# The input layer from token 1024 on as Strassen's seven block products, with weight sums streamed from device memory

## The chip, the cores and the metric

The kernel runs on one core of one Trainium2 chip. The metric is device time in microseconds: the median over several executions. A profile is of one execution, and its span runs from the first to the last instruction. Engines are named as in the profile: PE (TensorE matmuls), PEld (TensorE weight loads), DVE (VectorE), ACT (ScalarE), POOL (GpSimd), SP (SyncE, which issues most DMAs).

## The reference

Attention with 8 batches, 8 heads, 576 positions and head size 64, where four heads see a local window of 32 positions and four see positions with the same remainder modulo 32; its output is the input of a layer with three weight matrices, whose maximum goes through an output matrix:

```
scores = where(mask_of_head, (q @ k.T) / sqrt(64), -1e9)
attn   = softmax(scores)
x      = (attn @ v) as (8 * 576 tokens, 8 * 64 features)      # 4608 x 512
h      = maximum(maximum(x @ w1, x @ w2), x @ w3)             # w: 512 x 768
out    = h @ w_out                                            # 768 x 512
```

q, k, v are float32; the weights arrive as float64.

## The kernel before

Precision: TensorE multiplies in a reduced float32 ("float32r"). So each operand is split into a high part (the value rounded to that format) and a low part (what is left), and each product of a 128x128 block of weights with tokens is three matmuls: high x high, high x low, low x high. The weights are turned from 64-bit to 32-bit numbers and split on the chip, in the opening.

Attention is worked in 32 units (8 batches, 4 pairs of heads; pairs 2 and 3 strided, then 0 and 1 local). A unit's steps are `scores` (TensorE), `less_maximum` (DVE: mask, maximum, subtraction), `exponentials` (ACT), `probabilities` and `transposed` (DVE), `values` (TensorE), `leading` (ACT writes the high part of x) and `rest` (DVE writes the low part). From batch 1 on strided units also need `paired_queries`, four ACT copies. `load_qk` and `load_v` issue the unit's loads on SP.

The layer is worked in 9 chunks of 512 tokens, with features on the partitions, so that weights are the stationary operand. For each of 6 column blocks j and each of 3 matrices i, `ff_in` is a group of 12 matmuls (4 blocks of 128 features, three products each) of 512 columns into one of two accumulator banks; `ff_max` then takes it out: a copy by ACT for i = 0, a running maximum by DVE for i = 1 and 2, and then the split of the hidden layer (`hh` by ACT, `hl` by POOL). After the 18 groups `ff_out` makes four output tiles of 128 tokens, 18 matmuls of 512 columns each, which `ff_store` copies and stores.

Chunk 0 and the weights' conversion are in an opening whose order is written out by hand (`OPENING`: a letter for the step, a number for the unit, weight or group). The other chunks are a loop over 22 steps, with a burst of attention at the four steps in `BURSTS`:

```
if i in BURSTS and c < B - 1:
    n = 4 * (c + 1) + BURSTS.index(i)
    coming = n + 1 if n + 1 < len(units) else None
    values(n)
    if coming:
        scores(coming)
    list(load_v(n + 2)); leading(n); rest(n)
```

Each engine runs its instructions in this program order (`pin`); between engines, semaphores wait for data and for free buffers. A matmul group's first weight load carries the wait for its bank.

## Time and profile before

| | |
|---|---|
| median of 3 executions | 704.01 us (701.05 to 705.07) |
| span of the profiled execution | 701.0 us |
| PE busy | 677.7 us, 97% |
| weight loads (PEld) | 556.3 us, 79% |
| DVE, ACT, POOL busy | 295.7, 194.6, 151.1 us |
| moved by DMA | 55.67 MB, mean 79 GB/s |

The profile page has totals by engine, a picture of the span in 40 slices (busy tenths, the clock granted to TensorE, DMA), and the chain that ended last, followed back from the end. Groups of instructions are shown as "line engine operation out<-in shapes xcount | busy us, mean ns of one | idle time before them and who ended it". Answers by time show "start us, us, engine, line, operation".

### The profile page before, as it was taken

What the parts mean: (1) busy time and instruction counts of PE and PEld (TensorE: products, weight loads), DVE (VectorE), ACT (ScalarE), POOL (GpSimd) and SP (SyncE); (2) the same over time, 40 slices, a digit from 0 to 9 for tenths busy, and PEclk for the clock granted to TensorE, in tenths of its full rate; (3) what the DMA queues carried; (4) which work ended last, traced back from release to release, by engine and by line L of the source; (5) the groups of instructions that cost most, each with busy time, mean ns of one, the idle gap of its engine ahead of it and who ended that gap; (6) DMA issues with size and microseconds to landing.
All of it is one profiled execution on the core that took longest, in us unless ns stands there. A gap on an engine that the chain in (4) does not pass through costs nothing.

```text
span 701.0 us, 16767 instructions
## 1 busy us (share of the span) xinstructions
PE 677.7 (97%) x7408; PEld 556.3 (79%) x7408; DVE 295.7 (42%) x505; ACT 194.6 (28%) x440; POOL 151.1 (22%) x153
## 2 busy tenths in 40 slices
PE   3699999999999999999999999999999999999997
PEld 3577878888888888878888888888888888888886
DVE  5886963644435441555145534444255101101110
ACT  4666653212222222122222312222221111111111
POOL 8789880011001100011011100110010101100120
PEclk9999999999999999999999999999999999999999
DMA  8799123211312221222211232223120000010001
GB/s 289 195 291 364 48 84 110 74 56 65 107 54 75 66 81 47 69 84 64 84 56 56 68 108 70 57 65 94 54 54 2 31 31 1 0 46 15 1 1 60
DMA packets 36080, 55.67 MB, mean 79 GB/s; under 512 B 5256, under 2 KB 18568, under 8 KB 36008
## 3 DMA queue, kind: packets, MB, share of 16 engines
q1 hardware_dynamic: 30824, 45.17, 20.9%
q10 hardware_dynamic: 5184, 9.44, 3.6%
q8 instruction: 58, 0.95, 0.6%
q14 instruction: 14, 0.11, 0.0%
HBM read 45.15 MB, written 9.44 MB: 78 GB/s over the span
## 4 chain that ended last, share of the span: by engine, by line
PE 91%; DMA 5%; SPq 2%; DVE 1%; ACT 0%; issue 0%; DVEq 0%; ACTq 0%
PE f_ps L484 62%; PE f_ps L509 21%; DMA w<-in_w 5%; PE o_ps L405 2%; PE o_ps L435 2%; PE s_ps L292 2%; PE s_ps L314 2%; SPq L254 1%; SPq L140 0%; SPq L220 0%; SPq L247 0%; SPq L243 0%; DVE pt L378 0%; DVE s_ps L371 0%; DVE s_ps L368 0%
## 5 line engine op out<-in xcount | busy, mean ns | idle before, releaser
L484 PE MATMUL f_ps<-xh,w 128*128 128x512 f32 x1296 | 409.9, 393 | 0.9 <-ACT h_max L494 0.6
L484 PEld LDWEIGHTS f_ps<-xh,w 128*128 128x128 f32 x1296 | 244.3, 189 | 54.2 <-ACT h_max L494 1.0
L484 PE MATMUL f_ps<-xl,w 128*128 128x512 f32 x648 | 253.6, 391 | 0.4 <-DVE xl L467 0.4
L496 DVE TENSOR_TENSOR h_max<-f_ps,h_max 128x512 f32<-128x512 f32 x108 | 74.3, 688 | 287.9 <-PE f_ps L484 287.9
L500 POOL TENSOR_TENSOR hl<-h_max,hh 128x512 fp32r<-128x512 f32 x54 | 69.6, 1289 | 519.0 <-ACT hh L499 519.0
L484 PEld LDWEIGHTS f_ps<-xl,w 128*128 128x128 f32 x648 | 122.2, 189 | 25.3 <-DVE xl L467 0.7
L509 PE MATMUL f_ps<-wNone,hh 128*128 128x512 f32 x432 | 134.4, 392 | 0.3 <-issue 0.3
L509 PEld LDWEIGHTS f_ps<-wNone,hh 128*128 128x128 f32 x432 | 80.4, 188 | 16.8
L499 ACT CAST hh<-h_max 128x512 fp32r<-128x512 f32 x54 | 33.5, 620 | 202.6 <-DVE h_max L496 202.6
L509 PE MATMUL f_ps<-wNone,hl 128*128 128x512 f32 x216 | 84.1, 389 | 0.0
L467 DVE TENSOR_TENSOR xl<-o_ps,xh 128x320 fp32r<-128x320 f32 (+11 forms) x96 | 28.3, 350 | 53.9 <-ACT xh L463 47.0
L514 ACT COPY work<-f_ps 128x512 f32<-128x512 f32 x36 | 21.2, 589 | 101.5 <-PE f_ps L509 101.5
L494 ACT COPY h_max<-f_ps 128x512 f32<-128x512 f32 x54 | 31.7, 587 | 60.9 <-POOL hl L500 30.0
L509 PEld LDWEIGHTS f_ps<-wNone,hl 128*128 128x128 f32 x216 | 40.5, 188 | 9.1 <-issue 0.5
L358 ACT ACTIVATE s_ps<-s_ps 128x640 f32<-128x640 f32 (+2 forms) x30 | 19.4, 645 | 85.0 <-DVE s_ps L342 85.0
L378 DVE STREAM_TRANSPOSE pt<-s_ps 128x640 f32<-128x640 f32 (+2 forms) x32 | 32.4, 1013 | 0.7
L463 ACT CAST xh<-o_ps 128x320 fp32r<-128x320 f32 (+11 forms) x96 | 24.3, 328 | 25.4 <-PE o_ps L435 19.1
L314 PE MATMUL s_ps<-qk_t 64*32 64x64 f32 (+1 forms) x1408 | 20.0, 232 | 9.8 <-DMA qk_t<-in_kT 7.8
L314 PEld LDWEIGHTS s_ps<-qk_t 64*32 64x32 f32 x1408 | 16.7, 116 | 13.8 <-DMA qk_t<-in_qT 7.8
L337 DVE TENSOR_REDUCE mx<-s_ps 128x10 f32<-128x640 f32 (+2 forms) x32 | 24.7, 772 | 4.3 <-PE s_ps L314 3.3
L371 DVE TENSOR_TENSOR s_ps<-s_ps,sm 128x640 f32<-128x640 f32 (+2 forms) x32 | 25.0, 781 | 1.1
L184 POOL TENSOR_TENSOR work<-work,w 128x512 int32<-128x512 int32 x18 | 23.5, 1313 | 4.2 <-DVE sm L369 2.4
(55 smaller groups left out, 375.5 us busy)
## 6 DMA issues: line engine op xcount, KB each, us to landing
w<-in_w SPq DMA_DIRECT2D x18, 512.0 KB, 5.6
out<-work ACTq DMA_DIRECT2D x36, 256.0 KB, 2.0
qk_t<-in_qT SPq DMA_DIRECT2D x28, 288.0 KB, 3.4
qk_t<-in_kT SPq DMA_DIRECT2D x28, 288.0 KB, 3.6
v_t<-in_v_str SPq DMA_DIRECT2D x56, 128.0 KB, 3.3
v_t<-in_v_loc SPq DMA_DIRECT2D x48, 96.0 KB, 3.1
wNone<-in_w_out SPq DMA_DIRECT2D x6, 512.0 KB, 8.9
qk_t<-in_qk_str SPq DMA_DIRECT2D x4, 288.0 KB, 4.0
```

The lines of the kernel that those rows point to most:

```text
L314: pin(nc.tensor.matmul(s_ps[32 * j : 32 * (j + 1), h, k1 : k1 + w], t[hs, q0 : q0 + 32], t[hs, k0 : k0 + w], start=not first, stop=not fir ...
L337: pin(nc.vector.tensor_reduce(out=mx[:, :, :nm], in_=s, op=ALU.max, axis=axes))
L371: pin(nc.vector.tensor_tensor(out=s, in0=s, in1=wide(sm), op=ALU.mult))
L378: pin(nc.vector.transpose(pt[:, :, : nm * at], s_ps[:, :, : nm * at]))
L463: pin(nc.scalar.copy(out=hi, in_=src))
L467: pin(nc.vector.tensor_tensor(out=lo, in0=src, in1=hi.bitcast(F32), op=ALU.subtract))
L484: pin(nc.tensor.matmul(f_ps, w[:, kc, :], x[:, kc, :], start=(kc == 2 and n == 0), stop=(kc == 1 and n == 2)))
L494: pin(nc.scalar.copy(out=a, in_=f_ps))
L496: pin(nc.vector.tensor_tensor(out=a, in0=f_ps, in1=a, op=ALU.max))
L499: pin(nc.scalar.copy(out=hh, in_=a))
L500: pin(nc.gpsimd.tensor_tensor(out=hl, in0=a, in1=hh.bitcast(F32), op=ALU.subtract))
L509: pin(nc.tensor.matmul(f_ps, h[:, ts], w, start=(j == 0 and n == 0), stop=(j == NJ - 1 and n == 2)))
```

## The change

Chunks 0 and 1 (1024 tokens) stay as they were. The other 3584 tokens are eight blocks of 448; two neighbouring blocks make one of four rounds ("supers"). Within a round the input layer is a product of 2x2 blocks: two halves of the 512 features by two blocks of tokens, and for each matrix two neighbouring column blocks j, j + 1. Of the weights and of the tokens, sums and differences are formed (Strassen's method in Winograd's form), and seven block products of 2 x 3 matmuls of 448 columns take the place of eight. A "quad" (q = 0 to 8) is one pair of column blocks of one matrix: seven products into two accumulator banks that take turns. Each product but one is copied out by ACT (`snap`); a later product goes on adding onto the same bank, which forms part of the sums, and POOL adds the remaining pairs. DVE takes the maximum over the three matrices into one buffer `hall` of the whole round.

The sums of weights are built in the opening's end and in chunk 1 (`build_sums`, `build_mix`, `build_high`, `build_low`: mostly POOL), split in high and low and written to device memory. From there each product's weights (256 KB) are loaded by SP, eight products ahead. Attention's values for tokens from 1024 on, and for chunk 1, are copied whole (float32) by `leading`, without `rest`; `conversion` forms the sums of tokens and splits them during the output tiles of the round before (four pieces, in all seven ACT, nine DVE and two POOL operations 896 columns wide); `chunk_one` splits chunk 1.

Bursts of attention: eight instead of four in chunk 1 (two to three steps apart), then 6, 6, 4 and 0 in the four rounds, one in ten products; `values` and `scores` come ahead of a product, `exponentials` after the third, `probabilities` and `transposed` after the fourth, `paired_queries` after the sixth. `split` takes the place of `hh` and `hl`, partly ahead of the ninth quad's end. The output layer has the same number and size of matmuls.

```
-N7 H6 U8 L6 V7 Q1 Q2 H7 O3 Q3 L7 S8
...
+H5 D21 A23 F15 B22 N6 K22 C20 F16 K23 C21 L5 M15 M16 D22 B23 S7 D23 C22 C23 F17 V6 M17 Y0 X7 O0 G7 Q0 T2 T3 O1 O2
+N7 H6 U8 L6 Z0 V7 S8 Q1 Y1 T0 H7 X8 Q2 O3 E8 L7 T1 Q3 N8
...
+    def chunk_one(p):
+        raw, (hi, lo) = place_of(-1)[:, p, :], (x[:, p, :] for x in x_chunk(1))
+        pin(nc.scalar.copy(out=hi, in_=raw))
+        pin(nc.vector.tensor_tensor(out=lo, in0=raw, in1=hi.bitcast(F32), op=ALU.subtract))
...
+    def build_sums(q):
+        _, j, i = builds[q]
+        to = scratch[q].rearrange("p n (l f) -> p n l f", l=2)
+        for n in range(2):
+            pin(nc.sync.dma_start(out=to[:, A12 : A11 + 1, n], in_=halves(kept[i, j].bitcast(F32)[:, n])))
+        pin(nc.sync.dma_start(out=to[:, A22], in_=kept[i, j + 1].bitcast(F32)[:, :, :256]))
...
+        for x, jj, engine in zip(a, (j, j + 1), (nc.gpsimd, nc.gpsimd)):
+            parts = kept[i, jj].bitcast(F32)
+            pin(engine.tensor_tensor(out=x, in0=parts[:, 0], in1=parts[:, 1], op=ALU.add))
+
+    def build_mix(q):
...
+            pin(nc.gpsimd.tensor_tensor(out=out_, in0=x, in1=y, op=op))
+
+    def build_high(q):
...
+        for n, x in enumerate(a_of[q]):
+            pin(nc.scalar.copy(out=sh[:, n], in_=x))
+
+    def build_low(q):
...
+        for n, x in enumerate(a_of[q]):
+            pin(nc.gpsimd.tensor_tensor(out=x.bitcast(F32R), in0=x, in1=sh[:, n].bitcast(F32), op=ALU.subtract))
...
+    def burst(n, exponents_later=True):
+        values(n)
+        coming = n + 1 if n + 1 < len(units) else None
+        if coming:
+            scores(coming)
+        list(load_v(n + 2))
+        leading(n)
+        rest(n)
+        if coming:
+            list(load_qk(coming + 2))
+            less_maximum(coming)
+        return coming
+
+    def load_next():
+        if to_load:
+            _, q, m = to_load.pop(0)
+            w = second["wst"].tile([P, 2, 256], F32R, name="w_stream")
+            pin(nc.sync.dma_start(out=w.bitcast(F32), in_=scratch[q][:, m].rearrange("p (l f) -> p l f", l=2)))
+            stream.append(w)
+
+    def conversion(s):
...
+    first_bursts = {1: 8, 4: 9, 6: 10, 9: 11, 12: 12, 14: 13, 17: 14, 19: 15}
+    sums_at = {-2: 1, 0: 2, 3: 3, 5: 4, 7: 5, 9: 6, 11: 7, 14: 8}
+    for i in range(3 * NJ + CH // P):
+        if i in first_bursts:
+            coming, since = burst(first_bursts[i]), i
...
+        if i - 3 in sums_at:
+            build_high(sums_at[i - 3])
+            build_low(sums_at[i - 3])
+        if i in sums_at:
+            build_sums(sums_at[i])
+            build_mix(sums_at[i])
...
+        def product(out_, m, xm, w, start):
+            x = xm[m]
+            for k in range(2):
+                fs = slice(k * P, (k + 1) * P)
+                for n, (wl, xl) in enumerate(((0, 0), (0, 1), (1, 0))):
+                    pin(nc.tensor.matmul(
+                        out_, w[:, wl, fs], x[:, xl, k, :], start=start and k == 0 and n == 0, stop=k == 1 and n == 2, ...
+        def quad(s, q):
...
+            def go(out_, m, start=True):
+                before(s, k[0])
+                product(out_, m, x, stream.pop(0), start)
+                load_next()
+                after(s, k[0])
+                k[0] += 1
+            def snap(src):
+                t = second["snap"].tile([P, BL], F32, name="snap")
+                pin(nc.scalar.copy(out=t, in_=src))
+                return t
+            def out_of(src, t, jj, half_):
+                h = hall[:, jj, half_ * BL : (half_ + 1) * BL]
+                if t is None:
+                    if i == 0:
+                        pin(nc.scalar.copy(out=h, in_=src))
+                        return
+                    u = snap(src)
+                else:
+                    u = snap(src)
+                    pin(nc.gpsimd.tensor_tensor(out=h if i == 0 else u, in0=u, in1=t, op=ALU.add))
+                if i:
+                    pin(nc.vector.tensor_tensor(out=h, in0=h, in1=u, op=ALU.max))
+            go(a, A11)
+            s1 = snap(a)
+            go(c, S1)
+            s5 = snap(c)
+            go(a, S2, start=False)
+            s2 = snap(a)
+            go(c, S4, start=False)
+            out_of(c, s2, j, 1)
+            go(a, S3, start=False)
+            out_of(a, s5, j + 1, 1)
+            go(c, A12)
+            out_of(c, s1, j, 0)
+            go(a, A22, start=False)
+            out_of(a, None, j + 1, 0)
...
+        for s in range(NSUPER):
+            for q in range(9):
+                quad(s, q)
+                if q == 7:
+                    split(0, 0, 4, nc.gpsimd)
+                    split(1, 0, 4, nc.gpsimd)
+            split(2, 0, 4, nc.gpsimd)
+            split(0, 4, 6, nc.vector)
+            split(1, 4, 6, nc.vector)
+            split(2, 4, 6, nc.gpsimd)
+            convert = conversion(s + 1) if s + 1 < NSUPER else iter(())
+            out_part(0, 0, 4)
+            out_part(1, 0, 4)
+            for t in range(7):
+                out_part(t, 0 if t > 1 else 4, 6)
+                store(s, t)
+                if t < 4:
+                    split(t + 3, 0, 6, nc.gpsimd)
+                next(convert, None)
+            list(convert)
```

## The prediction, made before the change was run

> **What bounds the kernel now.** I read the page's totals first, then the chain that ended last, then the weight loads under the matmuls, then the waits of the engine that will empty the accumulators.

> ```profile
> span 701.0 us, 16767 instructions
> PE 677.7 (97%) x7408; PEld 556.3 (79%) x7408; DVE 295.7 (42%) x505; ACT 194.6 (28%) x440; POOL 151.1 (22%) x153
> PEclk9999999999999999999999999999999999999999
> PE 91%; DMA 5%; SPq 2%; DVE 1%; ACT 0%; issue 0%; DVEq 0%; ACTq 0%
> ```

> TensorE is busy in 97% of the span at its full granted clock and holds 91% of the chain. So time goes down only if TensorE has less to do, and comes back wherever it is made to wait. The chain in order of time gives the pace, with a burst of attention between matmuls and the two last chunks without any:

> ```profile
> 119.15 1.07 PE s_ps L292 x64
> 120.22 8.38 PE f_ps L484 x36
> 128.61 1.07 PE o_ps L435 x64
> 129.68 0.93 PE s_ps L292 x64
> 130.61 13.82 PE f_ps L484 x60
> ...
> 566.71 48.96 PE f_ps L484 x216
> 615.67 16.32 PE f_ps L509 x72
> 631.99 48.96 PE f_ps L484 x216
> ```

> 48.96 / 216 = 0.2267 us per 128x512 matmul, exactly the same in the output layer (16.32 / 72). With bursts it is 13.82 / 60 = 0.230. A burst is 1.07 + 0.93 to 1.07, some 2.1 us of TensorE. Chunk 1 begins at 120.22 and the last matmul ends at 697.3, so everything that changes lies in the last 577 us.

> **The term that is removed.** From token 1024 on, seven chunks had 18 groups of 12 input matmuls of 512 columns: 7 x 216 = 1512. Now there are four rounds (896 tokens each) of 9 x 7 products of 6 matmuls: 4 x 63 x 6 = 1512, of 448 columns. The count is the same; Strassen's eighth is in the width. Output matmuls stay (28 tiles x 18 = 504 of 512 columns), and so do the attention bursts: 24 from chunk 1 on, 8 now inside chunk 1, 16 in the rounds.

> No row has a 448-column matmul of this kind, so the pace is bounded: proportional it is 0.2267 x 448/512 = 0.1983 us, a gain of 1512 x 0.0284 = 42.9 us; if something per instruction sets the pace it stays 0.2267 and the gain is nothing. The suspect is the weight load, one for each matmul:

> ```profile
> L484 PEld LDWEIGHTS f_ps<-xh,w 128*128 128x128 f32 x1296 | 244.3, 189 | 54.2 <-ACT h_max L494 1.0
> ...
> 402.45 0.30 PEld L509 LDWEIGHTS f_ps<-wNone,hh 128*128 128x128 f32 x2
> 402.79 0.19 PEld L509 LDWEIGHTS f_ps<-wNone,hl 128*128 128x128 f32 x1
> ```

> A load lasts 189 ns, under 198. And where two follow each other with the array free (first row after a burst) they last 0.30 together, so the second began 0.30 - 0.19 = 0.11 us after the first: a load can hand over after 0.11 us, and its 189 ns are mostly latency. The third began only when the first 512 columns had streamed. So the stream sets the pace, and I take 0.1983: **-42.9 us**. [...]

> **What is added: the two-bank ring.** Before, a bank got 12 matmuls (2.72 us) and was then emptied once. Now each product of 6 x 0.1983 = 1.19 us is followed by an ACT copy of 448 columns ("snap"), and the product after next adds onto the same bank, so it must wait for that copy. The rows for it:

> ```profile
> 615.28 0.39 PE L484 MATMUL f_ps<-xh,w 128*128 128x512 f32 x1
> 615.50 0.62 PE L509 MATMUL f_ps<-wNone,hh 128*128 128x512 f32 x2
> 615.70 0.69 DVE L496 TENSOR_TENSOR h_max<-f_ps,h_max 128x512 f32<-128x512 f32 x1 [1.96 <-PE f_ps L484]
> L463 ACT CAST xh<-o_ps 128x448 fp32r<-128x448 f32 x4 | 2.1, 536 | 0.0
> 48.07 0.48 ACT h_max L494
> 48.60 0.98 PE f_ps L484 x3
> ```

> A reader starts 615.70 - 615.28 = 0.42 us after a group's last matmul began (0.49 in other places); a 448-wide copy out of the accumulators takes 0.536; TensorE resumed 0.05 us after ACT (48.55 to 48.60). One turn of a bank: 0.11 (load) + 5 x 0.198 + 0.45 + 0.54 + 0.05 = 2.14 us, against 2.38 for two products. It fits with 0.24 us to spare, so I cost it at nothing as long as ACT has nothing else. If ACT inserts other work between two snaps, 1.19 - 0.54 - 0.05 = 0.60 us are free, and with the 0.24 a piece of 0.84 us costs nothing. What ACT inserts:

> ```profile
> L358 ACT ACTIVATE s_ps<-s_ps 128x640 f32<-128x640 f32 x14 | 9.7, 690 | 41.8 <-DVE s_ps L342 41.8
> L269 ACT COPY pt<-qk_t 128x288 f32<-128x288 f32 x28 | 10.8, 442 | 0.0
> L269 ACT COPY pt<-qk_t 128x224 f32<-128x224 f32 x28 | 9.5, 391 | 0.0
> L499 ACT CAST hh<-h_max 128x512 fp32r<-128x512 f32 x54 | 33.5, 620 | 202.6 <-DVE h_max L496 202.6
> ```

> The exponential (0.69, after the third product of a burst) fits. The copies of the values stand under the burst's own 2.1 us. The paired queries are four copies, 2 x 0.442 + 2 x 0.391 = 1.67 us, 0.83 too many; units 20, 21, 24, 25, 28 and 29 have them inside the rounds: 6 x 0.83 = **+5.0 us** (0 if the next product absorbs it; 10 if it takes two snaps to recover). Two splits of the hidden layer in each ninth quad, 2 x 0.62 = 1.24: 4 x 0.40 = **+1.6 us**.

> **Chunk 1 with eight bursts.** The softmax of a unit must end before the next burst's values. Its rows, from the end of the scores at 130.61:

> ```profile
> 131.36 0.76 DVE L335 TENSOR_TENSOR s_ps<-s_ps,mpair 128x576 f32<-128x576 f32 x1
> 134.47 0.76 DVE L368 TENSOR_REDUCE sm<-s_ps 128x16 f32<-128x576 f32 x1 [0.76 <-ACT s_ps L358]
> 137.03 1.24 DVE L378 STREAM_TRANSPOSE pt<-s_ps 128x1024 f32<-128x1024 f32 x1
> ```

> It ends at 138.27, 7.66 us later. The first 0.75 (131.36 - 130.61) go to subtractions that the change takes out of the burst, since values from token 1024 on are copied whole and split later; about 0.15 of it stays as hand-over. So 7.06 us. Bursts stood five groups apart, now two or three: 3 x 2.72 = 8.2 holds it, 2 x 2.72 = 5.44 doesn't. Two gaps of two groups (steps 4 to 6, 12 to 14) cost 1.6 each; the first burst at step 1 follows the scores by 4.08 (output tile) + 2.72 = 6.8, and chunk one's own split (0.69 on DVE) is in between: 1.0. **+4.2 us**. The third close pair (17 to 19) has an output tile of 4.08 in it and fits.

> The sums are built on POOL here:

> ```profile
> L500 POOL TENSOR_TENSOR hl<-h_max,hh 128x512 fp32r<-128x512 f32 x54 | 69.6, 1289 | 519.0 <-ACT hh L499 519.0
> ```

> For each of nine weight pairs, 2 additions and 2 subtractions of 512 (1.29 each) and 4 of 256 (half, as an estimate 0.65): 7.8 us, eight of them in chunk 1 with its six "hl": 62 + 8 = 70 us in a stretch of 18 x 2.72 + 4 x 4.08 + 8 x 2.1 = 82 us. It fits, but at 85%, and ACT's high parts stand in order before the copies that free banks, so a late POOL operation holds TensorE. I take **+2 us**, ends 0 and 8. SP writes the parts out, 6 issues for a pair, and the loads of the next unit stand behind the writes that wait for POOL; those have a whole burst (over 5.4 us) to spare.

> The end of the opening gets chunk one's split (four ACT copies of 0.62, four DVE subtractions of 0.69), the first two weight pairs and unit 8's softmax, which before ran in chunk 1. POOL has nothing there:

> ```profile
> 130.06 1.29 POOL L500 TENSOR_TENSOR hl<-h_max,hh 128x512 fp32r<-128x512 f32 x1 [26.02 <-ACT hh L499]
> ```

> 26 us of idle POOL cover two pairs' sums and one pair's low parts (13 us), and the four output tiles (16.3 us) cover ACT and DVE; only the softmax before the first burst shows, and is priced above. On SP the six issues of pair 0 come ahead of unit 10's loads, which aren't due for 20 us.

> **The stream.** Each product loads 256 KB ahead by eight products (9.5 us). SP and the DMA engines carry it:

> ```profile
> 401.49 3.66 SPq L254 DMA_DIRECT2D v_t<-in_v_str  x4
> 405.26 0.52 SPq L220 DMA_DIRECT2D qk_t<-in_qT  x1
> 405.82 0.43 SPq L220 DMA_DIRECT2D qk_t<-in_kT  x1
> 620.40 0.34 ACTq L515 DMA_DIRECT2D out<-work  x1
> 17.50:35.00 17.50, 12.12 (x423) 8.84 (x429) 14.37 (x27) 12.08 (x37) 12.54 (x13) 1.00 0.72 196
> 52.60:70.00 17.40, 16.55 (x190) 13.37 (x189) 11.48 (x18) 12.07 (x24) 17.40 (x17) 1.00 1.06 366
> ```

> Ten products and a burst are 11.9 + 2.1 = 14.0 us. SP spends 3.66 + 0.52 + 0.43 = 4.6 on a unit's loads, which wait for TensorE's burst while the weights stand behind them, then 10 issues of 0.34 (the output's, same size) to 0.52: at most 9.8 of 14.0. Bytes: 10 x 262144 plus 576 + 512 KB of the unit are 3.74 MB, 267 GB/s, between the two windows' 196 (DMA engines 72% busy) and 366. Cost 0, covered by eight products of lead; without that cover see the rivals.

> **Between the rounds.** Output tiles (7 x 18 x 0.2267 = 28.6 us) cover the next round's conversion: on DVE nine operations of 896, as an estimate from the 512-wide 0.69 some 1.15 each, 10 us; on ACT seven copies, 6.5 us; on POOL six larger splits and two subtractions, 12 us. They are needed in order, the first product's first. I take **+3 us** over four rounds (0 to 12).

> **Sum.** 701.0 - 42.9 + 5.0 + 1.6 + 4.2 + 2 + 3 = 673.9 for the span. The profiled execution's span, 701.0, is the shortest of the three times (701.05); their median is 3.0 higher, and I keep this distance: **677 us**, 27 below 704.0. Less than 0.5% (3.5 us) could not be told from no change.

> **The rivals.**
> *The weight load or a per-instruction cost sets the pace* and 448 columns take 0.2267: 677 + 42.9 = 720, slower. For it: one load for every matmul, PEld at 79%. Against it: the second load 0.11 us after the first. It decides once the pace stays above about 0.216 (27 us of gain gone). Chance 0.05.
> *The ring binds.* Each 0.1 us by which a turn exceeds 2.38 costs 126 pairs x 0.1 = 12.6 us; at 2.60 the kernel is back at 704. For it: the margin is 0.24 us, and a snap also waits for one of eight buffers that POOL and DVE release. Against it: no other work of ACT comes between most snaps. I expect 695 to 708 where it holds; chance 0.09. [...]
> *The stream is late.* If SP needs over (14.0 - 4.6) / 10 = 0.94 us for a weight load, each 0.1 us more costs the 160 products with bursts 16 us: 1.2 us would give 677 + 42 = 719. If the DMA engines gave only 196 GB/s, a period would last 19.1 instead of 14.0, 16 x 5.1 = 82 us more, 759. Chance 0.05.
> *POOL late, beside DVE.* In the rounds DVE's maxima and conversions read two SBUF tensors while POOL does; before, one operand of DVE's came from the accumulators, and POOL kept its 1.29 us. If they had to take turns, the output stretch would hold 12 + 11 us in 28.6 and chunk 1's POOL would slip: the upper ends above, 8 + 12 instead of 2 + 3, give 692. Chance 0.14. [...]
> *All waits hidden*: 701.0 - 42.9 + 3 = 661, chance 0.02.

> **How the numbers follow.** The forecast (665 to 691) has 0.65. Range 665 to 702: it takes in late POOL and half of the ring's cases and leaves out the unchanged pace, the late stream, the other half of the ring and all hidden, some 0.17. Faster: 0.65 + 0.14 + 0.02 + a third of the ring's 0.09 = 0.84; same: another 0.04; slower: 0.12.

> **What would show it.** Right: input matmuls of the rounds start 0.198 to 0.200 us apart, 75 us for 378 of them without bursts; the weight loads' share near 90% or more; TensorE waits for ACT's snaps only behind paired queries and the splits; no wait of TensorE for the stream. Wrong: TensorE's largest wait in the rounds is for ACT copies of every product, or for the streamed weights; 448-wide matmuls at 0.22; chunk 1 longer than 82 + 7 us.

## The result: slower by 1.7%

The changed kernel takes 715.16 us (median of 4, 713.91 to 716.01) against 703.33 for the kernel before, a ratio of 1.0172 with a 95% interval of 1.0147 to 1.0198. Forecast were 677 us and a gain: the sign is wrong and the time lies above the range. The profiled execution has a span of 713.3 us, 39.4 above the sum's 673.9.

First the page of the changed kernel: totals, granted clock, DMA queue of the instructions, chain by engine, and two groups.

```profile
span 713.3 us, 18073 instructions
PE 657.0 (92%) x7408; PEld 563.7 (79%) x7408; DVE 374.7 (53%) x475; ACT 336.6 (47%) x702; POOL 379.2 (53%) x331
PEclk9689999999999899999999999999999998999999
q8 instruction: 59, 0.97, 0.6%
PE 75%; DVE 8%; DMA 7%; issue 4%; ACT 3%; SPq 2%; POOL 1%; ACTq 0%; DVEq 0%
L762 PE MATMUL f_ps<-xc,w_stream 128*128 128x448 f32 x1512 | 315.7, 369 | 4.7 <-ACT snap L800 3.7
L847 PE MATMUL f_ps<-wNone,h_parts 128*128 128x512 f32 x504 | 122.1, 405 | 9.3 <-ACT work L853 9.3
```

TensorE has 20.7 us less to do (677.7 before), yet its share fell from 97% to 92%: it waits 33 us more than before (713.3 - 657.0 against 701.0 - 677.7). Of the chain 91% was TensorE's, now 75%; DVE, ACT and "issue" have come in. The last two rows say where to look and where not: before the 1512 matmuls of the products TensorE idles 4.7 us in all, before the 504 output matmuls 9.3, all of it for ACT's copy of an output tile (L853).

Then the stretches: busy time of each engine, granted clock and DMA share for chunk 1, the way from it into round 0, the three boundaries between rounds, and round 3.

```profile
core 0: us, PE busy (x) PEld busy (x) DVE busy (x) ACT busy (x) POOL busy (x), PEclk, DMA share, GB/s
122.90:205.00 82.10, 72.62 (x1307) 58.97 (x1305) 50.07 (x72) 29.76 (x68) 65.28 (x64) 0.98 0.81 256
205.00:228.30 23.30, 17.80 (x252) 14.38 (x252) 11.55 (x14) 9.14 (x21) 2.19 (x1) 1.00 0.82 250
325.00:358.80 33.80, 30.68 (x133) 24.48 (x131) 19.31 (x14) 14.63 (x22) 18.47 (x10) 0.95 0.15 56
451.20:484.80 33.60, 30.50 (x130) 24.34 (x128) 19.19 (x14) 14.62 (x22) 18.28 (x9) 0.95 0.16 56
570.00:604.10 34.10, 30.97 (x124) 24.99 (x123) 18.35 (x14) 13.91 (x21) 17.27 (x9) 0.90 0.17 59
604.10:680.70 76.60, 76.60 (x379) 70.92 (x379) 22.13 (x22) 34.62 (x65) 35.24 (x29) 1.00 0.65 189
```

Round 3 (last row), which has no attention, is busy without a gap, and its weight loads fill 93%. The boundaries lose 3.1 us of TensorE each, and then some clock: 0.90 to 0.95 is the mean over 34 us. Chunk 1 loses 9.5 us, the way into round 0 5.5 up to 228.3 and more behind it.

The chain in order of time gives the pace: 76.61 / 378 = 0.2027 us for a matmul of 448 columns, 28.59 / 126 = 0.2269 for one of 512 (0.2267 before).

```profile
604.08 76.61 PE f_ps L762 x378
680.69 28.59 PE f_ps L847 x126
```

**A boundary.** TensorE, then ACT, DVE and POOL by time at the first one (the others look the same):

```profile
348.74 8.51 PE L847 MATMUL f_ps<-wNone,h_parts 128*128 128x512 f32 x29 [3.12 <-ACT work L853]
342.35 0.94 ACT L673 CAST xc<-x_block 128x896 fp32r<-128x896 f32 x1
347.26 0.94 ACT L673 CAST xc<-x_block 128x896 fp32r<-128x896 f32 x1 [3.98 <-DVE x_block L679]
348.11 0.58 ACT L853 COPY work<-f_ps 128x512 f32<-128x512 f32 x1
343.35 2.76 DVE L676 TENSOR_TENSOR xc<-x_block,xc 128x896 fp32r<-128x896 f32 x1
346.14 1.09 DVE L679 TENSOR_TENSOR x_block<-x_block,x_block 128x896 f32<-128x896 f32 x1
348.23 1.09 DVE L676 TENSOR_TENSOR xc<-x_block,xc 128x896 fp32r<-128x896 f32 x1 [1.00 <-ACT xc L673]
342.52 2.64 POOL L838 TENSOR_TENSOR h_parts<-h_all,h_parts 128x768 fp32r<-128x768 f32 x1 [1.05 <-ACT h_parts L837]
```

Read it from the bottom. POOL splits the hidden layer from 342.52 to 345.16. DVE's subtraction for a low part (L676), begun at 343.35 beside it, takes 2.76 us and ends at 346.11, 0.95 behind POOL; the same subtraction at 348.23, with POOL idle, takes 1.09. Only behind it can DVE make the next sum of tokens (L679, to 347.23), and ACT's high part of that sum (L673) starts at 347.26, after 3.98 us of waiting. Behind this conversion in ACT's order stands the copy of a finished output tile (L853, 348.11), and TensorE, which has filled both banks, stands still for 3.12 us.

**Into round 0.** ACT, with its queue of DMA issues:

```profile
213.03 0.59 ACT L557 COPY work<-f_ps 128x512 f32<-128x512 f32 x1 [0.65 <-PE f_ps L552]
218.93 0.34 ACTq L558 DMA_DIRECT2D out<-work  x1
219.31 0.95 ACT L673 CAST xc<-x_block 128x896 fp32r<-128x896 f32 x1 [5.69 <-DMA qk_t<-in_qT]
220.16 0.58 ACT L557 COPY work<-f_ps 128x512 f32<-128x512 f32 x1
```

ACT had copied an output tile by 213.62, but the issue of its store came out at 218.93, and ACT did nothing in between, although the conversion stood next. TensorE pays behind it: 3.29 us at 221.0 for unit 16's softmax, 0.96 at 227.9, and 3.72 at 230.4, where the third product of round 0 waits for a snap that stands behind the conversion. Behind it TensorE works at half clock (0.50 granted, from 233.5) until 240.3, which costs some 2.7 us.

**Chunk 1.** TensorE in its first burst:

```profile
127.29 0.78 PE L318 MATMUL s_ps<-qk_t,pt 64*64 64x36 f32 x38
131.22 0.88 PE L318 MATMUL s_ps<-qk_t,pt 64*64 64x36 f32 x25 [3.16 <-issue]
132.03 0.79 PE L522 MATMUL f_ps<-xh,w 128*128 128x512 f32 x1
```

TensorE stops in the middle of a unit's scores and waits for nothing that the profile shows ("issue"). Such stops in chunk 1 lose 3.36, 1.13 and 1.27 us, and 1.23 more just ahead of it (a loss is the time from one matmul's start to the next, less the usual distance). Each ends 1.3 to 1.5 us after a 16 KB piece of instructions has come in on the queue that the page calls q8 (here 128.85 to 129.77, by the DMA records, and TensorE resumes at 131.22). The third row is a matmul at half clock: 0.79 instead of 0.39.

### The profile page after: what moved, and what is told of

It reads as the page before. It is cut to its first block, busy times and chain, and to the rows that moved or that the text cites. A ratio compares the mean times of both kernels' runs of the same rounds, so it can differ in the third digit from the quotient of the medians.

```text
span 713.3 us, 18073 instructions
## 1 busy us (share of the span) xinstructions
PE 657.0 (92%) x7408; PEld 563.7 (79%) x7408; DVE 374.7 (53%) x475; ACT 336.6 (47%) x702; POOL 379.2 (53%) x331
## 4 chain that ended last, share of the span: by engine, by line
PE 75%; DVE 8%; DMA 7%; issue 4%; ACT 3%; SPq 2%; POOL 1%; ACTq 0%; DVEq 0%
PE f_ps L762 44%; PE f_ps L847 11%; PE f_ps L522 11%; DMA w<-in_w 5%; DVE x_block L679 3%; DVE xc L676 3%; PE o_ps L470 2%; PE o_ps L441 2%; PE f_ps L552 2%; PE s_ps L318 2%; PE s_ps L340 2%; ACT xc L673 1%; DMA scratch<-work 1%; DMA qk_t<-in_qT 1%; DMA scratch<-w 1%
## 5 line engine op out<-in xcount | busy, mean ns | idle before, releaser
L762 PE MATMUL f_ps<-xc,w_stream 128*128 128x448 f32 x1512 | 315.7, 369 | 4.7 <-ACT snap L800 3.7
L762 PEld LDWEIGHTS f_ps<-xc,w_stream 128*128 128x128 f32 x1512 | 283.9, 189 | 31.4 <-ACT snap L800 6.0
L800 ACT COPY snap<-f_ps 128x448 f32<-128x448 f32 x240 | 128.0, 534 | 161.7 <-PE f_ps L762 161.1
L814 DVE TENSOR_TENSOR h_all<-h_all,snap 128x448 f32<-128x448 f32 x96 | 95.7, 1034 | 124.2 <-POOL snap L812 124.2
L847 PE MATMUL f_ps<-wNone,h_parts 128*128 128x512 f32 x504 | 122.1, 405 | 9.3 <-ACT work L853 9.3
L847 PEld LDWEIGHTS f_ps<-wNone,h_parts 128*128 128x128 f32 x504 | 98.5, 196 | 32.1 <-ACT work L853 11.2
L522 PE MATMUL f_ps<-xh,w 128*128 128x512 f32 x288 | 96.3, 407 | 2.2 <-ACT xh L495 2.2
L522 PEld LDWEIGHTS f_ps<-xh,w 128*128 128x128 f32 x288 | 55.9, 194 | 16.7 <-ACT xh L495 2.6
L522 PE MATMUL f_ps<-xl,w 128*128 128x512 f32 x144 | 57.9, 402 | 2.3 <-issue 2.1
L676 DVE TENSOR_TENSOR xc<-x_block,xc 128x896 fp32r<-128x896 f32 x20 | 32.9, 1646 | 38.9 <-ACT xc L673 34.0
L673 ACT CAST xc<-x_block 128x896 fp32r<-128x896 f32 x28 | 25.6, 940 | 30.0 <-DVE x_block L679 23.9
L853 ACT COPY work<-f_ps 128x512 f32<-128x512 f32 x28 | 16.3, 584 | 41.7 <-PE f_ps L847 41.7
L676 POOL TENSOR_TENSOR xc<-x_block,xc 128x896 fp32r<-128x896 f32 x8 | 22.2, 2774 | 23.5 <-ACT xc L673 23.5
L522 PEld LDWEIGHTS f_ps<-xl,w 128*128 128x128 f32 x144 | 28.1, 195 | 7.7 <-issue 1.5
```

The costliest lines, as they stand in the source:

```text
L522: pin(nc.tensor.matmul(f_ps, w[:, kc, :], x[:, kc, :], start=(kc == 2 and n == 0), stop=(kc == 1 and n == 2)))
L673: pin(nc.scalar.copy(out=x[m][:, 0], in_=src))
L676: pin(engine.tensor_tensor(out=x[m][:, 1], in0=src, in1=x[m][:, 0].bitcast(F32), op=ALU.subtract))
L762: pin(nc.tensor.matmul(out_, w[:, wl, fs], x[:, xl, k, :], start=start and k == 0 and n == 0, stop=k == 1 and n == 2, skip_group_check=not ...
L800: pin(nc.scalar.copy(out=t, in_=src))
L814: pin(nc.vector.tensor_tensor(out=h, in0=h, in1=u, op=ALU.max))
```

## The experiments

**A finer conversion (fine_pieces).** Theory: the order on ACT makes the boundary stalls; DVE's next sum must be begun one output tile earlier. (Operations that follow each other stand on one line here.)

```
 low(A12, b21, nc.gpsimd)
-yield
 less(b11, b12, b11)
+yield
 high(S1, b11); low(S1, b11)
-yield
 high(S4, b22); less(b12, b22, b12)
+yield
+high(S3, b12)
 low(S4, b22); less(b22, b22, b11)
+yield
 high(S2, b22); low(S2, b22)
-yield
-high(S3, b12)
 less(b21, b21, b22)
+yield
```

> The conversion's same operations in five finer pieces, so that ACT's copy of a piece only needs what DVE got one output tile earlier. Theory (the output store of a tile stands in ACT's order behind a copy that waits for DVE): the three stalls of 3.3 us between output matmuls, and the half clock behind each (1.4 to 2.4 us), go; about 15 us less than the changed kernel's 715, so 700. Rival (the hidden layer's splits on POOL, or their three buffers, are late): the order of the copies is no matter, the stalls stay within 1 us, 713 to 716.

Measured 701.18 us; 0.9963 of the kernel before (0.9942 to 0.9984), 14 us less than the change as made. The boundary by TensorE, its stretch, and the two operations of DVE:

```profile
323.51 16.53 PE L848 MATMUL f_ps<-wNone,h_parts 128*128 128x512 f32 x72
340.62 11.63 PE L848 MATMUL f_ps<-wNone,h_parts 128*128 128x512 f32 x50 [0.58 <-ACT work L854]
320.00:354.00 34.00, 33.42 (x227) 27.50 (x226) 22.31 (x16) 16.90 (x26) 21.84 (x11) 1.00 0.23 75
L679 DVE TENSOR_TENSOR x_block<-x_block,x_block 128x896 f32<-128x896 f32 x12 | 30.7, 2561 | 0.3
```

0.58 instead of 3.12, and the clock stays at 1.00 through the stretch: the half clock belonged to the stall. DVE's sums are even slower here (2561 ns, 1540 in the change as made): the order is the cause, and the slow DVE only what it had no room for. The gain isn't evenly spread: from the first product to the last matmul the profiled execution is 18.6 us shorter (463.5 for 482.1), while it gets to the first product 3.7 us later, with more half clock in chunk 1.

**The same pieces without contention (split_on_dve).** The four splits of an output stretch go from POOL to DVE, which then has few POOL operations of two SBUF operands beside its own, but four operations more to do.

```
-split(t + 3, 0, 6, nc.gpsimd)
+split(t + 3, 0, 6, nc.vector)
```

> Pieces as in the changed kernel, but the four 768-wide subtractions of the hidden layer's splits between rounds go from POOL to DVE, so that POOL runs only the two subtractions of the conversion there. Theory (DVE's operations on two tensors in SBUF are stretched from 1.09 to 2.0 or 2.9 us while POOL runs one): DVE's operations stay near 1.1 except beside the conversion's own two on POOL, the copy that TensorE waits for comes 3 us earlier, and most of 15 us goes: 700 to 705. Rival (no contention; DVE's chain is just long): DVE has 4 x 0.85 us more per boundary ahead of the copies, so the stall grows from 3.3 to 5 or 6 us and the time to about 720.

Measured 708.82; 1.0084 (1.0066 to 1.0101). Between the two expectations. The sums by DVE, the change as made first:

```profile
L679 DVE TENSOR_TENSOR x_block<-x_block,x_block 128x896 f32<-128x896 f32 x12 | 18.5, 1540 | 0.2
```

```profile
L679 DVE TENSOR_TENSOR x_block<-x_block,x_block 128x896 f32<-128x896 f32 x12 | 13.0, 1086 | 0.1
345.56 2.79 PE L847 MATMUL f_ps<-wNone,h_parts 128*128 128x512 f32 x11 [2.43 <-ACT work L853]
```

The contention is real (1540 to 1086 ns), and taking it away shortens a stall by 0.7 us, net of the splits (0.96 to 1.30 us each by time) that DVE now has in its own order; the order alone is worth 2.5.

**Stores issued by SP (store_by_sp).** Theory: the store's issue holds ACT on the way into round 0.

```
-pin(nc.scalar.dma_start(out=out[...], in_=o_sb))               # ff_store
+pin((nc.sync if c else nc.scalar).dma_start(out=out[...], in_=o_sb))
```

> Chunk 1's four output stores are issued by SP instead of ACT; nothing else. Theory (ACT stood still for 5.3 us from 213.6 to 218.9 in front of a store's issue, until a load of the next unit had landed in a full queue, and conversion, paired queries and exponentials stood behind it): TensorE's stalls between 204 and 235 (2.4 + 3.5 + 1.1 + 3.9 us) shrink by 5 to 8 us, with the half clock of 2.4 us behind them: 705 to 710. Rival (DVE's conversion and the loads themselves are late): ACT waits as long for DVE instead, 713 to 717.

Measured 707.42; 1.007 (1.0039 to 1.0101), as expected. ACT goes straight from the copy to the conversion:

```profile
211.49 0.59 ACT L557 COPY work<-f_ps 128x512 f32<-128x512 f32 x1 [0.64 <-PE f_ps L552]
211.97 0.95 ACT L673 CAST xc<-x_block 128x896 fp32r<-128x896 f32 x1
227.38 6.85 PE L762 MATMUL f_ps<-xc,w_stream 128*128 128x448 f32 x26 [2.90 <-ACT snap L800]
```

The stalls at 204.8, 221.0 and 227.9 are gone or below 0.75 us; that of the third product stays at 2.9 (3.72).

**One weight pair instead of nine (one_pair_built).** Theory: the building's DMA traffic starves the instruction supply of chunk 1. Eight of nine pairs are neither built nor written; all products read the first.

```
 def build_sums(q):           # also build_mix, build_high, build_low
+    if q:
+        return
```

> Only the first of the nine weight pairs is built and written to device memory, and all rounds stream that one; the other eight pairs' POOL, ACT and SP work and their 14 MB of writes are left out of the opening and chunk 1. The layer's result is that of wrong weights; the matmuls and the streamed bytes of the rounds are the same. Theory (writes fill the DMA queues, so that TensorE's instruction fetches, the unit's loads and the stores come late): the stalls called issue (1.2, 3.4, 1.1, 1.3 us) in chunk 1 shrink to under 2 us together, and those between 204 and 235 to under 4, while the gaps in front of bursts two steps apart (1.8 and 2.3 us) stay: 697 to 702. Rival (chunk 1 loses to the softmax chain alone): 712 to 715.

Measured 704.1 in one run (span 702.4), above the theory's 697 to 702 and far below the rival's 712. The first burst's stop:

```profile
129.99 0.56 PE L318 MATMUL s_ps<-qk_t,pt 64*64 64x36 f32 x25 [1.18 <-issue]
```

The "issue" stops went from 7.0 to 3.9 us, not under 2: in the first burst 1.18 us is left of 3.16, the one at 185.7 all but goes, and the stops at 118.7 and 153.7 kept their 1.2 and 1.1. So the building's traffic or work lengthens such a stop and is not what makes it; and what the building costs by itself is within the 11 us that this kernel saves.

**The width of the products (widths).** What sets the pace: the columns alone, a fixed part, or the weight load? Rounds 1, 2 and 3 use only 256, 320 and 384 of the 448 columns; the rest of each product is left out.

```
+cols = (448, 256, 320, 384)[round_[0]]
-out_, w[:, wl, fs], x[:, xl, k, :], ...
+out_[:, :cols], w[:, wl, fs], x[:, xl, k, :cols], ...
```

> The changed kernel with the input matmuls of rounds 1, 2 and 3 cut to 256, 320 and 384 columns (448 in round 0); the other columns of these rounds are left out, all else is kept. It measures what sets the pace of 0.2027 us at 448. Theory A (columns at the slope between 448 and 512, 0.375 ns each, plus 35 ns): within a product 384 start about 0.179 us apart, 320 about 0.155, 256 about 0.131, the last two also held between products by the copies. Theory B (the weight load's 0.189 us and a hand-over set a floor near 0.200): 384, 320 and 256 all start about 0.19 to 0.20 us apart, and blocks narrower than 448 would gain nothing.

One run, span 684.2. Chain in order of time, round 3, and the weight loads:

```profile
585.64 58.28 PE f_ps L765 x336
L765 PEld LDWEIGHTS f_ps<-xc,w_stream 128*128 128x128 f32 x1512 | 243.2, 192 | 30.9 <-ACT snap L803 14.6 <-issue 7.1
L765 PE MATMUL f_ps<-xc,w_stream 128*128 128x256 f32 x378 | 55.5, 298 | 9.4 <-ACT snap L803 4.9 <-issue 3.8 <-DMA w_stream<-scratch 0.5
```

58.28 / 336 = 0.1734 for 384 columns. With 0.2267 for 512 that is a slope of 0.4164 ns a column and a fixed 13.5 ns. The line gives 0.1468 and 0.1201 for 320 and 256; the median distances of matmul starts there are 0.147 and 0.120. So a load of 192 ns is no floor, for a pace of 0.120 goes on under it, and neither theory had the law right. At 448 the line gives 0.2001, and 0.2027 was measured, in starts that lie 199 to 207 ns apart by turns in round 3 of the change as made, where nearly all of 512 columns lie 226 or 227 ns apart; why it alone lies 2.6 ns above stays open. The ring binds only at 256 columns, with 4.9 us of waits for snaps in a whole round; the 3.8 us of "issue" beside them are stops as in chunk 1.

**Both mends (both_fixes)**: the diffs of fine_pieces and store_by_sp.

> Finer conversion pieces and chunk 1's stores by SP together. If the two losses are separate (boundaries between rounds; the way from chunk 1 to round 0), the gains of 14 and 8 us add: 693, a ratio of 0.986 to the kernel before. If they are one loss (ACT held up anywhere lets the next wait show), the sum is smaller: 697 to 701.

Measured 696.33; 0.9892 (0.9868 to 0.9917). The first mend gained 14.0 and the second 7.7, both 18.8: not quite a sum, between the two expectations, and now 1.1% faster than the kernel before.

**Weights written out early (early_copies)**: both mends, and the parts that exist already are copied to device memory by SP in the opening, at nine places, rather than in chunk 1.

```
-    def build_sums(q):
+    def copy_parts(q):                   # step "W" of OPENING, W0 to W8
         ...
         pin(nc.sync.dma_start(out=to[:, A22], ...))
+    def build_sums(q):
```

> As both fixes, and the 27 copies of the split weights to device memory (6.9 MB of the 16 MB of writes) leave chunk 1 and the opening's end for the stretch of the opening from about 80 us on, where the DMA engines are little used. POOL's and ACT's building work stays where it is. Theory (full DMA queues make instruction fetches and loads late): the issue stalls in chunk 1 (about 1.2, 3.4 to 4.2, 0.4 to 1.1, 0.6 to 1.3 us) shrink by 3 to 6 us: 687 to 690. Rival (the building work itself holds TensorE up): the stalls stay and the time is within 2 us of both fixes.

Measured 697.65; 0.9923 (0.9896 to 0.995), no gain, as the rival had it. Chunk 1 in both_fixes, then here:

```profile
123.00:205.00 82.00, 74.70 (x1225) 61.20 (x1224) 50.24 (x74) 29.18 (x67) 64.32 (x64) 0.92 0.80 254
```

```profile
123.00:205.00 82.00, 71.79 (x1224) 57.95 (x1230) 48.90 (x71) 28.32 (x65) 64.47 (x64) 0.96 0.61 191
```

The DMA engines' share falls from 0.80 to 0.61, and the "issue" stops there are 1.8, 1.1 and 2.9 us: the first is shorter, the last longer than in the change as made. Emptier queues did not end them.

**All stores by SP (all_stores_by_sp)**: as early_copies, with chunk 0's stores on SP as well.

```
-pin((nc.sync if c else nc.scalar).dma_start(out=out[...], in_=o_sb))
+pin(nc.sync.dma_start(out=out[...], in_=o_sb))
```

> As early copies, and chunk 0's four stores also go to SP. Theory: ACT's wait of 1.9 us in front of the fourth store's issue (copy done at 123.7, issue at 125.5) goes, and the values of unit 8 and the first accumulator copy of chunk 1 come earlier: 1 to 2 us less than early copies. Rival: SP issues them behind the first pair's sums, so the buffers that the second and third pair's sums need come free later: 1 to 4 us more.

Measured 695.83; 0.9897 (0.9864 to 0.993), 1.8 us less than early_copies, with ranges that overlap (693.43 to 698.86, 695.9 to 699.91): told neither from early_copies nor from both_fixes.

**The conversion first (split_first)**: both mends, and in chunk 1's last three output tiles ACT's and DVE's conversion stands ahead of unit 16's softmax; a round's bursts move from products 0, 10, ... to 2, 12, ..., so that the first two products do not wait for that softmax.

```
+if i > 3 * NJ:
+    ff_store(1, i - 3 * NJ)
+    next(convert, None)
 if coming and i == since:
     exponentials(coming)
...
-if k % 10 == 0 and k // 10 < COUNTS[s]:
+if k % 10 == 2 and k // 10 < COUNTS[s]:
```

> Both fixes, and in chunk 1's last three output tiles the conversion's pieces come ahead of unit 16's softmax on ACT and DVE; the bursts in the rounds start at the third product instead of the first, so that unit 16 isn't needed at once. Theory (the 3.7 us stall at the third product of round 0, and the 0.9 us before it, are DVE doing softmax and conversion in the wrong order): both stalls together fall under 1.5 us, the half clock behind them (2.3 us) goes: 690 to 693. Rival (DVE has more work there than time, whichever comes first): the stall moves to the values of unit 16 at the third product, 695 to 698.

Measured 693.07 (691.61 to 693.58) against 704.17; 0.9853 (0.9831 to 0.9876): with the next one the best version, 1.5% faster than the kernel before. Two lines of the page, and TensorE at the start of round 0 and behind the first boundary's stall:

```profile
span 689.9 us, 18068 instructions
PEclk9679999999999999999999999999999999999999
220.87 2.59 PE L767 MATMUL f_ps<-xc,w_stream 128*128 128x448 f32 x12
226.38 5.94 PE L767 MATMUL f_ps<-xc,w_stream 128*128 128x448 f32 x28 [0.91 <-ACT snap L805]
331.01 12.53 PE L852 MATMUL f_ps<-wNone,h_parts 128*128 128x512 f32 x54 [0.59 <-ACT work L858]
```

Round 0's products start straight behind the last output tile, the wait at a boundary is 0.59 us, and behind the opening's first three slices (52 us) the clock falls below 9 in none. The run moved the bursts and the conversion together, so it doesn't tell what each is worth.

**Two subtractions to POOL (split_first_pool)**: the same, and in round 0's conversion two low parts by POOL.

```
-low(A11, b11)
+low(A11, b11, nc.vector if s else nc.gpsimd)      # and S1 likewise
```

> As split first, and two more subtractions of round 0's conversion go from DVE to POOL, which is idle there. If DVE's amount of work is the limit, 2 us less than split first. If POOL's operations on two tensors in SBUF stretch DVE's beside them as between the rounds (1.09 to 2 us and more), nothing or 1 to 2 us more.

Measured 693.07; 0.985 (0.9823 to 0.9877): no gain. DVE's sums now wait for POOL:

```profile
L679 DVE TENSOR_TENSOR x_block<-x_block,x_block 128x896 f32<-128x896 f32 x12 | 30.8, 2570 | 5.7 <-POOL xc L676 5.4
```

**Fewer instructions at the same traffic (half_bursts)**: the change as made, without the small matmuls of one of two heads in chunk 1's bursts.

```
-for h in range(2):                          # scores and values
+for h in range(1 if 9 <= n < 16 else 2):     # values: 8 <= n < 16
```

> The changed kernel with only one of the two heads' small matmuls in chunk 1's bursts (values of units 8 to 15, scores of 9 to 15; the other head's are left out): about half of the 256 to 300 instructions that TensorE takes in 2 us there. All DMAs are kept. The stalls called issue end 1.4 to 1.5 us after one 16 KB piece of TensorE's instructions has come through the DMA engines. Theory (a burst takes instructions faster than their pieces come; full queues only lengthen it): the stalls of 3.4, 1.1 and 1.3 us in chunk 1 go or stay under 0.5 each, besides 8 us less of small matmuls: 701 to 704 in all, with the 1.2 us stall ahead of chunk 1 as it was. Rival (the full DMA queues alone): the stalls stay at 3 to 6 us together, 706 to 708. In both cases the gaps of 1.8 and 2.3 us in front of bursts two steps apart grow by up to 1 us each, since the softmax then waits less for its scores but TensorE is done sooner.

One run: 716.46, where 701 to 704 was expected by the instruction theory. On the stops it is right: from 118 to 140 us TensorE's clock stays at 1.00 and no "issue" stop is left in chunk 1, at a DMA share of 0.82 where the change as made had 0.78. Windows, the change as made first:

```profile
118.00:140.00 22.00, 17.29 (x186) 13.78 (x186) 12.60 (x18) 5.84 (x13) 12.23 (x13) 0.92 0.78 246
```

```profile
118.00:140.00 22.00, 20.50 (x204) 16.45 (x203) 15.31 (x21) 8.79 (x19) 15.46 (x16) 1.00 0.82 261
356.20 0.30 PE L340 MATMUL s_ps<-qk_t 64*32 64x64 f32 x3 [1.85 <-issue]
q8 instruction: 55, 0.90, 0.5%
```

On the time it is wrong. Chunk 1 ends some 6 us earlier (its last output matmul at 215.3 for 221.4) and the first product starts 4.0 us earlier, not the 11 to 14 of the theory, in part because a gap of 2.06 us in front of a burst is now followed by 6.83 us of half clock (from 176.4). Then stops of the same kind turn up inside bursts of the rounds, where the change as made has one above 0.7 us (0.9 at 307.6): 2.05 us at 354.1, 2.35 at 415.7 and 1.33 at 501.0, with some 3 us of half clock behind the first two. So the stops moved with the count of instructions ahead of them.

The count itself can be read from the traces. TensorE's matmuls, its weight loads and its sequencer's instructions are 15120 records in the change as made, 14048 here and 14893 in the kernel before, and the page's q8 brought 59, 55 and 58 pieces: 255 to 257 records a piece. The number of records that begin before the matmul that ends a stop is 3522, 3777, 4545, 5570 and 8641 in the change as made, 3522, 8386, 9922 and 11457 here, and 962 and 2241 in the kernel before. Each of these eleven is 193 or 194 more than a multiple of 256. In the change as made and in the kernel before they are all the stops of over 0.9 us, start to start, that the profile calls "issue" from 20 us on. (Left out is the gap at 180.7: the profile calls it "issue" too, but it ends with DVE's transposition, which is done at 182.72, 0.10 us before TensorE goes on, in the change as made.) So I take a stop to stand where one piece ends and the next begins. Most ends of pieces passed without one: 59 pieces and five such stops in the change as made. The stops came where TensorE had taken the instructions ahead fast, in a burst or close behind it: a burst has as many as a piece, 2 x 128, in 2.1 us, where the pieces ahead of these stops took 0.9 to 1.1 us to come and, in the change as made, TensorE went on 1.3 to 1.5 us later; a piece of long matmuls lasts some 125 x 0.2 = 25 us, as an estimate. This last part, why some ends of pieces stopped TensorE and others didn't, is argued and was not tried by itself.

## Why the prediction was wrong, and where it was right

The excess of 39.4 us over the sum, term by term (stalls by the starts of TensorE's matmuls; half clock by the time at half clock behind a stall, of which a 512-wide matmul loses 0.47, as its starts lie 0.427 us apart there in place of 0.227):

| | predicted | measured | excess |
|---|---|---|---|
| pace of 448 columns | -42.9 | 1512 x (0.2267 - 0.2027) = -36.3 | 6.6 |
| opening, start of chunk 1 (120.22, now 122.87) | 0 | 2.7, of it 1.23 "issue" | 2.7 |
| chunk 1 (122.87 to 221.2, of 82.1) | 6.2 | 16.2: softmax 4.7, "issue" 5.8, half clock 1.6, wait for ACT at 204.8 2.4, rest 1.7 | 10.0 |
| into round 0 | 0 | 3.5 + 1.1 + 3.9 + 0.3 + half clock 2.7 | 11.5 |
| paired queries, splits, other stalls in rounds | 6.6 | 2.3, by difference | -4.3 |
| three boundaries | 3 | 3 x 3.3 + half clock 6.0 | 12.9 |
| sum | | | 39.4 |

**The step that failed first: "Between the rounds".** It added up DVE's, ACT's and POOL's work (10, 6.5 and 12 us) against 28.6 us of output matmuls, found room, and took 3 us. At the first boundary they came to 15.0 us for DVE's nine operations, 6.6 for ACT's seven and 15.3 for POOL's four whole splits and two subtractions: the prediction was too low for two of the three, but all stay far below 28.6, so the room was there. It was beside the point: the engines do this work in turns, in an order that also holds ACT's copies which free TensorE's accumulator banks. Between two such copies lay ACT's high part of S4, three operations of DVE, and ACT's high part of S2, each waiting for the one before, with POOL in DVE's way. fine_pieces shows it: same work, another order, 14 us less.

**The step that was missing: into round 0.** The page of before has no such passage, and I priced the conversion only where output tiles of a round cover it. In chunk 1's last tiles the same conversion stands beside a unit's softmax, its queries and SP's loads, and 11.5 us came of it, with 2.4 just ahead. store_by_sp and split_first show the parts: a DMA issue that held ACT (the store on SP ends the stalls but that of the third product), then the order on ACT and DVE, which split_first changed together with the place of the bursts.

**The price that I did not know: TensorE's own supply of instructions.** Eight bursts in chunk 1 where four stood; four stops of 1.1 to 3.4 us, 7.0 in all. half_bursts and the count of records (193 or 194 past a multiple of 256, eleven times) put them at the ends of pieces of instructions; one_pair_built shows that the one in the first burst is longer beside the building of the weights (3.16 us, and 1.18 with one pair).

**The stall's second price.** After five of the six stalls of over 3 us from 120 us on TensorE worked at half clock (0.50 granted) for a while: some 10 us in all. Nothing in the trace of before past the opening stalls so long, and its granted clock is 1.00 from 100 to 689 us. In the changed kernel the granted clock changed at steps of 3.41 us behind the opening, and half clock lasted one step or two (3.41 or 6.83 us). The five steps that came ahead of half clock held 3.05, 2.80, 2.58, 2.31 and 2.21 us in which TensorE was idle; the stall at 221.4 is as long as those at the boundaries, but a step ends inside it, its two parts are 1.88 and 1.41 us, and full clock went on. From 100 us on to the last 12 us no other step at full clock of this trace held more than 1.88 us of idle time, and none of them was followed by half clock. What sets the clock is not shown.

**The pace was mis-sized, not misjudged.** Proportional scaling took the fixed 13.5 ns of a matmul (the line through 384 and 512 columns in widths) to shrink with its columns. Of the 6.6 us this is 1512 x 13.5 ns x 64/512 = 2.6, and the 2.6 ns that 448 columns lie above the line are the other 4.0. The rival of an unchanged pace is refuted: 0.2027 us against 0.2267.

**Right:** the ring (4.7 us of idle time before all 1512 matmuls of the products, none behind most snaps); the stream (no stall of TensorE for it); the softmax gaps of chunk 1, 1.79 + 2.28 + 0.65 = 4.7 for 4.2; round 3 without a gap, with its loads at 93%. The paired queries and the splits were priced too high: the next product absorbs them, the end that the prediction named at 0. POOL in chunk 1 held nothing up (2 us priced).

**The rival of a late POOL beside DVE** named the right resource: the same subtraction of DVE's took 1.09 us with POOL idle and 2.76 beside POOL's split. That the two would be in each other's way was an assumption ahead of the run. But the rival priced it as a lack of room, at 12 us between rounds and 692 us in all, and fine_pieces keeps the contention and loses the stalls. Of what was to show the forecast wrong, one sign came: chunk 1 longer than 89 us (98.3).

## What to carry to other kernels

When work is moved beside a matmul stream, do not compare sums of busy time: write down, for each engine, what stands in order between two of its copies that free an accumulator bank, and count how often the chain crosses to another engine in between. Give each such chain one more tile of lead, and keep DMA issues that may be held off the engine that frees the banks. A stall near 3 us cost up to 1.8 times itself here (3.3 and 2.8 of half clock), one below 1 us only itself.

## What was not expected of the hardware

- A float32r matmul with its weight load took 13.5 ns and 0.4164 ns a column from 256 to 512 columns (0.120, 0.147 and 0.1734 us in widths, 0.2267 in the kernel before), but 448 columns took 0.2027, 2.6 ns more.
- TensorE stopped for 1.1 to 3.4 us in a run of small matmuls, or close behind one, while a 16 KB piece of instructions came in; in chunk 1 of the changed kernel it resumed 1.3 to 1.5 us after the piece. The eleven stops counted above stand at 193 or 194 records past a multiple of 256. The kernel before had such stops too, of 0.93 and 0.85 us, at 25.9 and 64.7 us.
- Beside an operation of POOL's on two SBUF operands DVE's with two was stretched: in the four cases of the first boundary DVE's operation on 128x896 (1.09 us alone, 1.7 to 2.9 here) ended 0.94 to 0.95 us behind POOL's, however long it had stood. One of the four, by time (336.84 + 2.90 = 339.74, and 335.82 + 2.97 = 338.79):

```profile
335.82 2.97 POOL L676 TENSOR_TENSOR xc<-x_block,xc 128x896 fp32r<-128x896 f32 x1
336.84 2.90 DVE L679 TENSOR_TENSOR x_block<-x_block,x_block 128x896 f32<-128x896 f32 x1
```
